# Attention with part of the exponentials on VectorE: batches opened more densely, closed early, and worked in halves

## The chip, the cores and the metric

The kernel runs on one core of a Trainium2 chip. The metric is the device time of one execution in microseconds, the median over several runs. Five engines each work through a list of their own, in order: TensorE (PE, with its weight loads as PEld), VectorE (DVE), ScalarE (ACT), GpSimd (POOL) and SyncE (SP, which issues nearly all DMAs).

## The reference

The input x has 2048 rows of 640 numbers (bf16). Two branches read it and a gate mixes them:

```python
g = sigmoid((x * gate_w).sum(-1, keepdims=True))
# A: attention, 32 heads of 20, scale 20 ** -0.5
q, k, v = heads(x @ wqkv)
p = softmax(einsum("bhqd,bhkd->bhqk", q, k) * scale)
a = merge(einsum("bhqk,bhkd->bhqd", p, v)) @ wo
# B: dense 640 -> 1536 -> 640 with mish
h = x @ w1 + b1
b = (h * tanh(softplus(h))) @ w2
out = g * a + (1 - g) * b
```

The attention has 32 x 2048 x 2048 scores, and each needs an exponential. That is the bulk of the work outside TensorE.

## The kernel before, in words

**How it is tiled.** The queries are cut into four chunks `c` of 512, the heads into eight groups `g` of four. A pair (c, g) is a group of the schedule; there are 33, because the last pair is cut into two of 256 queries. For each group and each of 16 key tiles of 128 keys, the scores of one head fill one PSUM bank: 128 keys x 512 queries in fp32. That is one unit; there are 2048. No maximum is subtracted; a check on the size of q and k, made while the kernel runs, would send it to a second, safe program that is not executed with these inputs.

**Slots.** Three banks make a slot, and 683 slots make the attention. `emit_s` (line 1086) writes a slot's scores (`score_mms`, line 1107, matmuls at line 1117) into one of two sets of three banks, so the scores of slot s + 2 wait until slot s has been read. `emit_e` (line 1128) issues one ScalarE exponential per slot over all its banks (line 1139, PSUM to the ring `ETS` of five slots in bf16). `pv` (line 1349, matmuls at line 1363) multiplies V with the exponentials, four heads at a time, and sums a group's output in one PSUM bank (ACC). When a group's last tile has been multiplied, `group_done` (line 1399) copies ACC to `OUNG` (line 1444), has the row sums inverted (line 1451, with DMAs around it) and scales (line 1412).

**Banks that VectorE takes.** In some slots ScalarE reads only two banks, and VectorE takes the third: `emit_x` (line 1181, instruction at line 1184) turns the scores into 16-bit integers whose bits, read as bf16, are a rough exponential F. Up to four such banks of one group, each of another head, make a batch and lie in a pad, a piece of memory that happens to be free. When the batch is closed (`close`, line 1199), five more VectorE steps follow for the whole batch: two masks (line 1240) split mantissa and exponent E, an affine map of the mantissa (line 1244), its square (line 1249) and the product with F (line 1254), which gives a correction U. TensorE then multiplies V with F, E and U, so one bank taken this way costs three bank passes of a batch in place of one (`emit_off`, line 1319). Pads come from `take_pad`: two of their own (`PADS`), two work areas, and regions lent until their owner needs them: a half of `HB` and the key tiles of the last two head groups (`LENT`, regions k 6 and k 7 of `KT`); later parts of `QT` and `OTN`.

**What sets the order.** Nothing is scheduled on the chip. A planner in the kernel (`attention`) walks through the slots with its own cost for each instruction and writes every engine's list, with semaphore waits between them. Around this change it works as follows.

- `choose(s)` (line 1272) says whether slot s gives a bank to VectorE. Before the change it refuses when the slot before gave one, when VectorE's lag behind ScalarE and its queued work together reach `BEHIND` = 7 us, when too few pads are free, or, for a new batch, when the group's end is nearer than `FILL` + `CHAIN` (5 + 5 us) and the queued work. It takes a unit of the group, of a head that is in neither the slot nor the batch.
- A batch is closed when it has four banks, or when its group has no unit left for it.
- `close` puts the five steps as pieces into one of two lanes; `work(until)` (line 434) picks pieces that fit before the next fixed instruction of VectorE.
- Other work goes between: tasks for the projections (`pack_task`, `pack_end_task`, `v_pair_task`), the dense branch (`h_task` with its eviction at line 901, `mish` with a ScalarE tanh at line 924 and four VectorE steps at line 942, `b_task` evicted at line 957) and the output projection (`p_task`, `part_task`, matmuls at line 974, evictions at line 980). Tasks marked forced are put in at their due slot whatever else waits (line 1666). `fill_up` puts in spare matmuls (line 1642) where TensorE's list would be thin.

Of the kernel before, what the change touches and what calls it, by code (L numbers as in the profile page):

```python
# [9 lines left out]
BF16 = mybir.dt.bfloat16  # L10
I32 = mybir.dt.int32
I16 = mybir.dt.int16
FP16 = mybir.dt.float16
# [24 lines left out]
SLOT = 3  # L38
# [17 lines left out]
WIDE = 0.60  # L56
FAST = 0.335
HALVED = 0.41
LANES = 2
TAKEN = 3.6  # L60
LATE_OFF = 0.8
# [163 lines left out]
def bass_gated_mix__softmax_full_mha__dense_activation_mish__prompt_kernel(  # L225
# [141 lines left out]
    def attention(pl, fast):  # L367
# [831 lines left out]
        def close():  # L1199

            batch = open_batch[0]
            if batch is None or len(batch["evs"]) < len(batch["units"]):
                return
            open_batch[0] = None
            lane = soon[n_batches[0] % LANES]
            n_batches[0] += 1
            y, m = batch["y"], len(batch["units"])
            evs = list(batch["evs"])
            batch["parts"]["F"] = evs[-1]
            got = {}  # L1210
            group = batch["group"]
            ends = max((i for i, v in enumerate(islice(order, 80)) if v[:2] == group), default=0)
            if place[order[0][:2]] < place[group] if order else False:
                ends += NKT * HG
            due = pl.now["act"] + ends / TAKEN * EXP

            def piece(cost, fns, deps, after=None):
                def run():
                    for fn in fns():
                        op = pl.add("dve", fn, deps(), cost=cost * m / BATCH / len(spans(m)) if len(spans(m)) > 1 else cost if m == BATCH else cost * m / BATCH + 0.03)  # L1220
                    after(op)
                lane.append((cost, run, lambda: latest_of(deps()), due))

            def latest_of(ops):
                ops = [op for op in ops if op is not None]
                return max(ops, key=lambda op: op.t1) if ops else None

            def reserve():
                def run():
                    batch["u"], got["u"] = take_pad(batch)  # L1230
                    batch["E"], got["E"] = take_pad(batch)
                lane.append((0.0, run, lambda: None if len(free_pads()) >= 2 else False, due))

            def step(name):
                def after(op):
                    got[name] = op
                return after

            def masked(to, mask):
                return lambda: [lambda e, sp=sp: e.tensor_scalar(  # L1240
                    some_of(batch[to], sp, I16), some_of(y, sp, I16), mask, None, ALU.bitwise_and) for sp in spans(m)]

            def affine():
                return [lambda e, sp=sp: e.tensor_scalar(
                    some_of(batch["u"], sp, FP16), some_of(batch["u"], sp, I16), FIT_AT / 128, FIT_AT + FIT_TO,
                    ALU.mult, ALU.add) for sp in spans(m)]

            def square():
                return [lambda e, sp=sp: e.tensor_tensor(  # L1249
                    some_of(batch["u"], sp, FP16), some_of(batch["u"], sp, FP16), some_of(batch["u"], sp, FP16),  # L1250
                    ALU.mult) for sp in spans(m)]

            def times_f():
                return [lambda e, sp=sp: e.tensor_tensor(
                    some_of(batch["u"], sp, BF16), some_of(batch["u"], sp, FP16), some_of(y, sp, BF16),
                    ALU.mult) for sp in spans(m)]
# [12 lines left out]
            piece(DOUBLE, square, lambda: [got["a"]], step("s"))  # L1269
            piece(DOUBLE, times_f, lambda: [got["s"]], end)  # L1270

        def choose(s):

            late = max(0.0, pl.now["dve"] - pl.now["act"])
            urgent, other = (sum(t[0] for todo in some for t in todo) for some in ((norm, *soon), (blend, bg)))
            if len(order) < SLOT or late + urgent + other >= BEHIND or s - 1 in off:
                return None
            js = [v[3] for v in islice(order, 2)]
            near = list(islice(order, 80))
            batch = open_batch[0]  # L1280
            if batch is None:
                group = near[2][:2]
                ends = max(i for i, v in enumerate(near) if v[:2] == group)
                left = ends / TAKEN * EXP
                before = sum(t[0] for t in blend if t[3] < pl.now["act"] + left)
# [15 lines left out]
            top = NKT  # L1301
# [359 lines left out]
        for step in range(NSLOT + 40):  # L1661
# [227 lines left out]
```

## Time and profile before

| | |
|---|---|
| median of 3 runs | 850.33 us (849.99 to 850.58) |
| the profiled execution | 851.44 us, of which the trace spans 849.6 us |
| granted TensorE clock, mean | 0.991 |
| busy: PE, DVE, ACT | 747.2, 738.8, 825.0 us |
| ScalarE exponentials (line 1139) | 683, of them 403 over three banks and 280 over two |
| banks taken by VectorE (line 1184) | 279 (the last slot has only two banks) |

How to read it: a row of a group view gives line, engine, operation, output <- input, shapes and count, then busy time, the mean length of one instruction, and the idle time of the engine just before, with what ended it. An engine's instructions overlap at their ends, so the busy time of a group is less than count times mean; the distance from start to start is what an instruction costs its engine. The view of windows gives busy time of each engine in a stretch, the granted share of the TensorE clock (PEclk), the busy share of the DMA engines and GB/s. In the timeline a row has start, length, engine, line and what it waited for.

### The profile page before, as it was taken

How to read it: one execution, taken by the hardware profiler on the slowest of the kernel's cores; microseconds unless marked ns; L12 is line 12 of the kernel's file. 1: busy time of each engine (PE TensorE's matmuls, PEld its weight loads, DVE VectorE, ACT ScalarE, POOL GpSimd, SP SyncE). 2: the span in 40 equal slices, each digit the busy share in tenths (PEclk: the TensorE clock that was granted, in tenths of full speed). 3: DMA queues.
4: the chain of work that ended last, by engine and by line, in shares of the span. 5: the costliest groups of instructions: out<-in, count | busy, mean ns of one | idle time of the engine just before them, and what ended most of it. 6: DMA issues, size and time to landing. Idle time of an engine off the chain costs nothing.

```text
span 849.6 us, 16334 instructions
## 1 busy us (share of the span) xinstructions
PE 747.2 (88%) x6813; PEld 265.5 (31%) x6853; DVE 738.8 (87%) x1052; ACT 825.0 (97%) x714; POOL 7.3 (1%) x14
## 2 busy tenths in 40 slices
PE   8889999889888889899888998889998989899884
PEld 3333333233222332233223333333333333233231
DVE  4678788999999998778968899979999999999884
ACT  6999999999999999999999999999999999999983
POOL 3000000000000000000000000000000000000000
PEclk9999999999999999999999999999999999999997
DMA  9721310221223221411111221112212121000001
GB/s 216 96 60 44 105 50 12 73 58 50 67 82 97 79 58 49 125 39 31 33 54 36 65 61 47 30 39 59 76 35 66 44 76 46 10 26 22 18 15 35
DMA packets 78180, 48.47 MB, mean 57 GB/s; under 512 B 23964, under 2 KB 73748, under 8 KB 78052
## 3 DMA queue, kind: packets, MB, share of 16 engines
q1 hardware_dynamic: 75732, 46.87, 20.9%
q8 instruction: 56, 0.92, 0.4%
q10 hardware_dynamic: 2256, 0.47, 0.3%
q0 software_dynamic: 112, 0.01, 0.1%
q14 instruction: 24, 0.20, 0.1%
HBM read 37.64 MB, written 7.52 MB: 53 GB/s over the span
## 4 chain that ended last, share of the span: by engine, by line
ACT 93%; PE 3%; DVE 2%; DMA 1%; issue 0%; SPq 0%; ACTq 0%
ACT ETS L1139 90%; ACT REG L924 2%; PE PS L1117 1%; ACT W2R L924 1%; PE PS L1363 1%; DMA RR<-OUNG 1%; DMA OTN<-in_A_x_dram 1%; PE PS L891 0%; PE PS L974 0%; PE PS L1642 0%; DVE HB L980 0%; PE PS L719 0%; PE PS L772 0%; DVE KT L1249 0%; PE PS L710 0%
## 5 line engine op out<-in xcount | busy, mean ns | idle before, releaser
L1139 ACT ACTIVATE ETS<-PS 128x1536 bf16<-128x1536 f32 (+1 forms) x683 | 807.5, 1507 | 6.2 <-PE PS L1363 3.9
L1117 PE MATMUL PS<-QT,KT 32*128 32x512 bf16 (+1 forms) x2161 | 272.1, 378 | 81.5 <-ACT ETS L1139 65.7
L1363 PE MATMUL PS<-ETS,V_all 128*21 128x512 bf16 (+1 forms) x1818 | 188.1, 379 | 0.3 <-ACT ETS L1139 0.3
L1117 PEld LDWEIGHTS PS<-QT,KT 32*128 32x128 bf16 x2161 | 67.7, 91 | 288.4 <-ACT ETS L1139 251.2
L1363 PEld LDWEIGHTS PS<-ETS,V_all 128*21 128x21 bf16 x1818 | 48.8, 89 | 81.2 <-issue 76.0
L950 PE MATMUL PS<-W2R,HB 128*128 128x320 bf16 x384 | 71.9, 302 | 0.4 <-DVE HB L901 0.2
L1184 DVE TENSOR_SCALAR PADS<-PS 128x512 int16<-128x512 f32 x88 | 60.2, 684 | 12.8 <-PE PS L1117 12.4
L891 PE MATMUL PS<-XB,REG 128*128 128x256 bf16 x360 | 57.6, 279 | 0.9 <-DVE HB L901 0.5
L1184 DVE TENSOR_SCALAR QT<-PS 128x512 int16<-128x512 f32 x56 | 38.4, 685 | 14.0 <-PE PS L1117 13.7
L1184 DVE TENSOR_SCALAR OTN<-PS 128x512 int16<-128x512 f32 x67 | 45.7, 682 | 5.4 <-PE PS L1117 4.8
L901 DVE TENSOR_TENSOR HB<-PS,B1T 128x512 bf16<-128x512 f32 x48 | 32.8, 683 | 10.3 <-PE PS L891 10.0
L950 PEld LDWEIGHTS PS<-W2R,HB 128*128 128x128 bf16 x384 | 29.0, 97 | 36.1 <-issue 25.0
L891 PEld LDWEIGHTS PS<-XB,REG 128*128 128x128 bf16 x360 | 28.3, 98 | 28.6 <-issue 26.3
L1363 PE MATMUL PS<-PADS,V_all 128*21 128x512 bf16 (+1 forms) x278 | 27.6, 372 | 0.6 <-DVE PADS L1240 0.6
L1249 DVE TENSOR_TENSOR PADS<-PADS 128x2048 f16<-128x2048 f16 x23 | 27.9, 1219 | 0.2
L974 PE MATMUL PS<-WOQ,QT 128*128 128x320 bf16 x128 | 25.6, 313 | 0.5 <-issue 0.3
L974 PE MATMUL PS<-WOQ,OTN 128*128 128x320 bf16 x128 | 24.0, 302 | 0.7 <-DVE OUTT L980 0.6
L772 PE MATMUL PS<-REG,XB 128*128 128x160 bf16 (+1 forms) x240 | 24.2, 234 | 0.1
L639 PE MATMUL PS<-XB,REG 128*128 128x512 bf16 x71 | 22.5, 384 | 1.6 <-issue 0.8
L924 ACT ACTIVATE REG<-HB 128x1024 f32<-128x1024 bf16 x18 | 23.8, 1322 | 0.0
L1444 DVE COPY OUNG<-PS 128x512 f32<-128x512 f32 x31 | 21.2, 684 | 2.7 <-PE PS L1363 2.4
L942 DVE SCALAR_TENSOR_TENSOR U<-REG 128x1024 f32<-128x1024 f32 x18 | 21.9, 1218 | 0.8 <-ACT REG L924 0.8
(193 smaller groups left out, 835.5 us busy)
## 6 DMA issues: line engine op xcount, KB each, us to landing
REG<-in_B_w_dram SPq DMA_DIRECT2D x36, 320.0 KB, 3.1
BCT<-SUMS SPq DMA_DIRECT2D x124, 64.0 KB, 2.1
W2R<-in_B_w_dram SPq DMA_DIRECT2D x12, 320.0 KB, 3.3
KT<-KS SPq DMA_DIRECT2D x28, 128.0 KB
QT<-QS SPq DMA_DIRECT2D x112, 20.0 KB
QS<-WOQ SPq DMA_DIRECT2D x16, 128.0 KB, 1.7
KS<-OTN SPq DMA_DIRECT2D x16, 128.0 KB, 1.7
W2R<-in_B_w_dram SPq DMA_DIRECT2D x1, 1920.0 KB, 10.2
```

The lines of the kernel that those rows point to most:

```text
L639: return lambda e, bank: e.matmul(PS[:, bank, :], W[:, f, base:base + P], xt(c)[:, f, :], start=(f == 0), stop=(f == NFT - 1))
L772: return lambda e, bank: e.matmul(PS[:, bank, i * n:(i + 1) * n], xt(t // 4)[:, f, t % 4 * P:(t % 4 + 1) * P], WV[:, f, g * HD:g * HD + n] ...
L891: return lambda e, bank: e.matmul(PS[:, bank, i * HW:(i + 1) * HW], w1b(n1)[:, f, i * P:(i + 1) * P], xt(c)[:, f, cols], start=(f == 0), s ...
L901: ev = dve(lambda e: e.tensor_tensor(hb, PS[:, bank, :].rearrange("p (i t) -> p i t", i=2), bias, ALU.add), [last, b_load, *guarded, *b_re ...
L924: ex = pl.add("act", lambda e: e.activation(U, h, AF.Tanh, scale=0.5, bias=-MISH_AT / 2), [ev, u_free[0]], cost=0.95)
L950: return lambda e, bank: e.matmul(PS[:, bank, 0:HALF], HB[:, hc % 2, f, t * P:(t + 1) * P], W2[:, f, half * HALF:(half + 1) * HALF], start ...
L974: return lambda e, bank: e.matmul(PS[:, bank, 0:HALF], otn(c, g, fast)[:, t * P:(t + 1) * P], WOG[:, g, half * HALF:(half + 1) * HALF], st ...
L1117: op = pl.add("pe", lambda e, i=i, g=real(g), tile=tile, j=j, cols=cols, c=c, of_q=of_q: e.matmul(scores(s)[:, i, cols], KT[32 * j:32 * j ...
L1139: e_op[s] = pl.add("act", lambda e: e.activation(ETS[:, s % NETS, 0:n, :], scores(s)[:, 0:n, :], AF.Exp, scale=SCALE, bias=LIFT if fast el ...
L1184: ev = dve_by(lambda e: e.tensor_scalar(block(batch["y"], n, I16), scores(s)[:, 2, :], SCALE * ULPS, BIAS, ALU.mult, ALU.add), [s_op[s], * ...
L1249: return [lambda e, sp=sp: e.tensor_tensor(some_of(batch["u"], sp, FP16), some_of(batch["u"], sp, FP16), some_of(batch["u"], sp, FP16), AL ...
L1363: lasts[n] = pl.add("pe", lambda e, tile=tile, h=real(g) * HG + j, j=j, src=src[:, cols], of_q=of_q, count=count: e.matmul(PS[32 * j:32 * ...
```

## The change

It touches the planner only; every kind of instruction stays, and the lists come out in another order and number.

1. **Pace.** A slot may give a bank although the slot before did, if few of the last four did (`crowded`); three in a row only where VectorE's queue is under 1.5 us. A new batch is opened as long as 2.5 + 2.5 us, the margin and the queued work fit before the group's end (`FILL` halved, half of `CHAIN`).
2. **Closing.** Where the group's end comes near, an open batch is closed with one, two or three banks.
3. **Halves.** The two products of a batch of four (square and product with F) may run as two instructions of half the size, where the whole would not fit before VectorE's next fixed instruction.
4. **Lent pads.** For forced tasks `ready()` is called from 30 slots before they are due, which withdraws the lent pads k 6 and k 7 from the list of open pads that much earlier.

In the built lists this makes of 279 banks in 71 batches (69 of four, one of two, one of one) 303 banks in 79 batches (68 of four, nine of three, two of two). Of the 68 batches of four, 38 squares and 44 products are issued in halves. ScalarE has 379 exponentials over three banks and 304 over two. VectorE's list grows by 191 instructions. TensorE gets 48 more full-size V matmuls; its spare matmuls of line 1642 go from 67 to 49, and its scores of line 1117 from 2161 to 2154. SP has the same 475 instructions in another order, POOL the same 20 in the same order.

```diff
-FILL = 5.0
+FILL = 2.5
+PACE = 4
+GIVE_BACK = 30
+IDLE = 1.5
+HALF_WORK = 0.60
...
@@ work
+                        halve = len(todo[0]) > 4 and begin + cost > until
+                        if halve:
+                            cost = HALF_WORK
                         if begin + cost <= until and (best is None or begin < best[0] - 0.01):
-                            best = (begin, todo, fn)
+                            best = (begin, todo, fn, halve)
...
+                if best[3]:
+                    todo = best[1]
+                    halves = todo[0][4]
+                    todo.popleft()
+                    todo.extendleft(reversed(halves))
+                    todo.popleft()[1]()
+                    continue
@@ close
-            def piece(cost, fns, deps, after=None):
...
+            def piece(cost, fns, deps, after=None, split=False):
+                def run(some, each, mark):
+                    def go():
+                        for sp in some:
+                            op = pl.add("dve", fns(sp), deps(), cost=each)
+                        if mark:
+                            after(op)
+                    return go
...
+                if split and m == BATCH:
+                    parts = [(0, 1, 0, 2), (1, 2, 0, 2)]
+                    entry += ([(HALF_WORK, run([sp], HALF_WORK, n == 1), after_deps, due) for n, sp in enumerate(parts)],)
+                lane.append(entry)
...
-            piece(DOUBLE, square, lambda: [got["a"]], step("s"))
-            piece(DOUBLE, times_f, lambda: [got["s"]], end)
+            piece(DOUBLE, square, lambda: [got["a"]], step("s"), True)
+            piece(DOUBLE, times_f, lambda: [got["s"]], end, True)
+        def crowded(s, todo):
+            lately = sum(s - i in off for i in range(1, PACE + 1))
+            return s - 1 in off and lately > (1 if todo >= IDLE else 2)
@@ choose
-            if len(order) < SLOT or late + urgent + other >= BEHIND or s - 1 in off:
+            if len(order) < SLOT:
                 return None
...
+            def tight(group, need):
+                ends = max((i for i, v in enumerate(near) if v[:2] == group), default=0)
+                left = ends / TAKEN * EXP
+                before = sum(t[0] for t in blend if t[3] < pl.now["act"] + left)
+                return (late + urgent + before) * CROWD + need + MARGIN >= left
+            batch = open_batch[0]
+            if batch and place[near[2][:2]] >= place[batch["group"]] and tight(
+                    batch["group"], CHAIN * (len(batch["units"]) + 1) / BATCH):
+                close()
+            if late + urgent + other >= BEHIND or crowded(s, late + urgent + other):
+                return None
...
-                if (late + urgent + before) * CROWD + FILL + CHAIN + MARGIN >= left:
+                if tight(group, FILL + CHAIN / 2):
@@ main loop, each step
+            for t in tasks:
+                if t.forced and t.due - GIVE_BACK <= step:
+                    t.ready()
```

More of the change, by code (lines that the diff above doesn't have):

```diff
@@ L1215, in close @@
             due = pl.now["act"] + ends / TAKEN * EXP
-            def piece(cost, fns, deps, after=None):
[L1218 to L1222, printed above, removed]
+            def piece(cost, fns, deps, after=None, split=False):
[6 more added lines that the diff above has]
+                    return go
+                where = spans(m)
+                each = cost * m / BATCH / len(where) + (0.0 if m == BATCH else 0.03)
+                after_deps = lambda: latest_of(deps())
+                entry = (each * len(where), run(where, each, True), after_deps, due)
+                if split and m == BATCH:
+                    parts = [(0, 1, 0, 2), (1, 2, 0, 2)]
+                    entry += ([(HALF_WORK, run([sp], HALF_WORK, n == 1), after_deps, due) for n, sp in enumerate(parts)],)
+                lane.append(entry)
             def latest_of(ops):
@@ L1239, in masked, with affine, square, times_f @@
             def masked(to, mask):
[L1240 to L1244, printed above, removed]
+                return lambda sp: lambda e: e.tensor_scalar(
+                    some_of(batch[to], sp, I16), some_of(y, sp, I16), mask, None, ALU.bitwise_and)
+            def affine(sp):
+                return lambda e: e.tensor_scalar(
                     some_of(batch["u"], sp, FP16), some_of(batch["u"], sp, I16), FIT_AT / 128, FIT_AT + FIT_TO,
[L1246 to L1256, printed above, removed]
+                    ALU.mult, ALU.add)
+            def square(sp):
+                return lambda e: e.tensor_tensor(
+                    some_of(batch["u"], sp, FP16), some_of(batch["u"], sp, FP16), some_of(batch["u"], sp, FP16), ALU.mult)
+            def times_f(sp):
+                return lambda e: e.tensor_tensor(
+                    some_of(batch["u"], sp, BF16), some_of(batch["u"], sp, FP16), some_of(y, sp, BF16), ALU.mult)
             def end(op):
@@ L1282, in choose @@
                 group = near[2][:2]
-                ends = max(i for i, v in enumerate(near) if v[:2] == group)
-                left = ends / TAKEN * EXP
-                before = sum(t[0] for t in blend if t[3] < pl.now["act"] + left)
-                if (late + urgent + before) * CROWD + FILL + CHAIN + MARGIN >= left:
+                if tight(group, FILL + CHAIN / 2):
                     n = place[group] + 1
@@ L1300, in choose @@
             js += [u[3] for u in batch["units"]]
-            top = NKT
             mine = [v for v in near[2:] if v[:2] == group and v[3] not in js and v[2] < tiles(*group) - 1]
```

## The prediction

> **What bounds the kernel now.** I read the page first (shares, chain), then the groups by form, the chain in order of time, the windows of 50 us, the waits, and the timeline where ScalarE stopped. The page:
>
> ```profile
> span 849.6 us, 16334 instructions
> PE 747.2 (88%) x6813; PEld 265.5 (31%) x6853; DVE 738.8 (87%) x1052; ACT 825.0 (97%) x714; POOL 7.3 (1%) x14
> ...
> ACT 93%; PE 3%; DVE 2%; DMA 1%; issue 0%; SPq 0%; ACTq 0%
> ```
>
> ScalarE is busy 97% of the span and holds 93% of the chain. So what a bank costs ScalarE is what moving it is worth, as long as nothing makes ScalarE wait. Two groups by form, and three pieces of the chain in order of time (start, length, what):
>
> ```profile
> L1139 ACT ACTIVATE ETS<-PS 128x1536 bf16<-128x1536 f32 x403 | 637.0, 1680 | 3.4 <-PE PS L1363 1.8 <-PE PS L1117 1.5
> L1139 ACT ACTIVATE ETS<-PS 128x1024 bf16<-128x1024 f32 x280 | 352.2, 1258 | 2.8 <-PE PS L1363 2.1 <-PE PS L1117 0.6
> ...
> 327.48 0.94 ACT W2R L924
> 328.41 77.20 ACT ETS L1139 x67
> 405.61 0.94 ACT REG L924
> ```
>
> The means differ by 1.680 - 1.258 = 0.422 us. In the piece of 67 exponentials 30 are over two banks (counted in the built list), so one over three costs (77.20 + 30 x 0.422) / 67 = 1.341 us and one over two 0.919 us. All of ScalarE's stream is then 403 x 1.341 + 280 x 0.919 + 24 tanh x 0.94 = 820.3 us. The rest of the span is start (the first exponential is at 9.8 us), end, and few waits: 6.2 us before the exponentials, of which 3.9 us behind L1363 lie at the end (below).
>
> VectorE is the next limit, and not evenly:
>
> ```profile
> 300.00:350.00 50.00, 43.38 (x390) 14.12 (x394) 45.56 (x66) 50.00 (x45) 0.00 (x0) 1.00 0.33 94
> 350.00:400.00 50.00, 46.09 (x399) 15.12 (x397) 39.05 (x59) 50.00 (x45) 0.00 (x0) 1.00 0.11 29
> 500.00:550.00 50.00, 44.39 (x383) 16.04 (x379) 48.72 (x65) 50.00 (x45) 0.00 (x0) 1.00 0.16 45
> 600.00:650.00 50.00, 45.31 (x403) 16.88 (x399) 49.25 (x65) 50.00 (x45) 0.00 (x0) 1.00 0.22 60
> 700.00:750.00 50.00, 46.24 (x398) 16.42 (x394) 48.73 (x66) 50.00 (x45) 0.00 (x0) 1.00 0.13 36
> ```
>
> Columns are PE, PEld, DVE, ACT, POOL. VectorE has 39 us of work in one window and 49 in another, and ScalarE is at 50.00 in all: a VectorE that is 98.5% busy (600 to 650) did not stop it.
>
> **The change, part by part.**
>
> *ScalarE.* 24 banks more leave it (303 against 279): 24 x 0.422 = 10.1 us less, 810.2 us of stream. That is the whole gain that the change can bring. Where they come from: before slot 100 seven, slots 100 to 350 ten, 350 to 600 eight, behind it one less.
>
> *VectorE.* What an instruction costs is the distance between starts:
>
> ```profile
> 799.86 0.68 DVE L1184 TENSOR_SCALAR OTN<-PS 128x512 int16<-128x512 f32 x1
> 800.46 0.68 DVE L1412 TENSOR_TENSOR QT<-OUNG,BCT 128x512 bf16<-128x512 f32 x1
> 801.06 1.22 DVE L1249 TENSOR_TENSOR OTN<-OTN 128x2048 f16<-128x2048 f16 x1
> 802.20 0.68 DVE L1184 TENSOR_SCALAR OTN<-PS 128x512 int16<-128x512 f32 x1
> ...
> 836.73 0.62 DVE L1240 TENSOR_SCALAR PADS<-OTN 128x1024 int16<-128x1024 int16 x2
> 837.26 0.62 DVE L1244 TENSOR_SCALAR OTN<-OTN 128x1024 f16<-128x1024 int16 x2
> 837.92 1.03 DVE L1249 TENSOR_TENSOR OTN<-OTN 128x1024 f16<-128x1024 f16 x2
> 838.98 1.03 DVE L1254 TENSOR_TENSOR OTN<-OTN 128x1024 bf16<-128x1024 f16 x2
> ```
> ```profile
> L1249 DVE TENSOR_TENSOR OTN<-OTN 128x1024 f16<-128x1024 f16 x1 | 0.7, 693 | 0.0
> ```
>
> An eviction or a mask over four banks takes 0.60 us, a product 1.14, so about 0.08 less than its length, and a half product 0.693 - 0.083 = 0.61. The tail shows a batch of three: 0.54 per mask or map, 0.95 per product (1.03 - 0.08), and 0.12 more where an instruction follows its own producer (837.26 to 837.92 is 0.66). The sum: 24 evictions 14.4; 82 halved products x (2 x 0.61 - 1.14) = 6.6; nine batches of three x (3 x 0.54 + 2 x 0.95) = 31.7; one batch of four less, -4.1; the small batches about +0.9. Together +49.5 us: 738.8 becomes 788 in a shorter span, 94% busy in place of 87%. Bank for bank that is 2.06 us of VectorE for 0.42 us of ScalarE.
>
> I laid these costs on both built lists between the same evictions. ScalarE against VectorE, us: slots 5 to 100, before 111.8 and 84.0, after 111.5 and 97.2; 100 to 350, before 296.3 and 262.9, after 289.8 and 277.1; 350 to 600, before 310.3 and 283.3, after 306.9 and 303.2. Cut into five, that last stretch has after the change ScalarE 60.6, 60.2, 64.6, 60.1, 61.5 and VectorE 60.1, 57.9, 64.4, 59.1, 61.8. So VectorE's free time goes from 27 to under 4 us there; the cover that hid its work is gone.
>
> *What comes back as waits.* VectorE's list also holds evictions that must wait for TensorE, so it can't be 100% busy. In the three fullest windows above it idles 1.28, 0.75 and 1.27 us of 50, 2.2% on average. If that share stays, each stretch of 50 slots takes 1.022 times its VectorE work or its ScalarE work, whichever is longer: 0.8 + 1.2 + 0.2 + 1.7 = 3.9 us over ScalarE in slots 351 to 601, none elsewhere. With no idle time it is 0.3 us; with 4% it is 10.4 us, of which 2.0 in slots 102 to 300 (at 97% before any idling). I take 3.9, the measured share; halved products make idle gaps smaller, which speaks for less, and the next point for more.
>
> *Two in a row.* 41 times two, 4 times three neighbouring slots give a bank (never before). The scores of slot s + 2 wait for both readers of slot s, and have one exponential of 0.92 in place of 1.34 us to be made in. How tight it is:
>
> ```profile
> 460.40 0.68 DVE L1184 TENSOR_SCALAR PADS<-PS 128x512 int16<-128x512 f32 x1
> ...
> 461.23 0.39 PE L1117 MATMUL PS<-QT,KT 32*128 32x512 bf16 x3 [0.69 <-DVE PADS L1184]
> ```
>
> There the eviction, not ScalarE, released the scores. Before, ScalarE lost 2.1 us to late scores (L1117) in all. Bounds: nothing, to 49 x 0.42 = 20.6 us if every place was just in time. I take it as part of the 3.9 us, since VectorE catches up while ScalarE waits; alone, at 0.06 us a place, it would be 3.
>
> *TensorE.* 24 more passes of a batch at 0.22 to 0.40 us are 5 to 10 us; 18 spare matmuls less give back 5 (L1642: 16.9 us for 57). [...]
>
> ```profile
> 462.00:464.00 2.00, 1.92 (x11) 1.12 (x11) 1.95 (x3) 2.00 (x3) 0.00 (x0) 0.62 0.00 0
> 464.00:466.00 2.00, 2.00 (x14) 0.44 (x12) 1.16 (x2) 1.31 (x2) 0.00 (x0) 0.53 0.00 0
> ...
> 464.84 1.02 ACT L1139 ACTIVATE ETS<-PS 128x1024 bf16<-128x1024 f32 x1 [0.56 <-PE PS L1117]
> 466.27 2.37 ACT L1139 ACTIVATE ETS<-PS 128x1536 bf16<-128x1536 f32 x2 [0.40 <-PE PS L1117]
> ```
>
> The granted clock fell once, to 0.62 and 0.53, and ScalarE waited 0.96 us. [...]
>
> *The end.* ScalarE waits 2.13 and 1.78 us for the last full group:
>
> ```profile
> 824.51 0.40 PE L1363 MATMUL PS<-REG,V_all 128*21 128x256 bf16 x8
> 825.15 2.37 ACT L1139 ACTIVATE ETS<-PS 128x1024 bf16<-128x1024 f32 x2 [2.13 <-PE PS L1363]
> 829.30 7.74 ACT L1139 ACTIVATE ETS<-PS 128x1536 bf16<-128x1536 f32 x6 [1.78 <-PE PS L1363]
> ```
>
> The V matmul at 824.51 waited for that group's last product. In the after list one eviction (slot 675) stands behind this product and no longer before it: 0.6 us earlier. The rest of the end has the same instructions, one of L980 moved across.
>
> *Pads, SP, POOL.* Withdrawing k 6 and k 7 earlier leaves fewer homes; what that costs is already in the count of 303. SP's 475 instructions are the same, reordered with the groups; POOL's list is the same: 0. A group's inversion DMAs could hold a VectorE step; such waits were 3.1 us in all (L1451), the ring of five slots covers them.
>
> **Sum.** -10.1 + 3.9 - 0.6 = -6.8 us. The profiled execution took 851.44 us, 1.1 above the median of 850.33; it would be 844.6, the median 843.5.
>
> **Rivals.**
> (a) The gain stays whole: the halves fill every gap and VectorE idles nowhere. -10.1 + 0.3 - 0.6 gives 839.9. For it: 49.25 of 50 us without a stop. Against: five stretches at 96 to 101%.
> (b) VectorE becomes the bound and takes the gain back: at 4% idle, +10.4 gives 850.0. For it: before, no stretch of 50 slots was over 97%.
> (c) Slower: in the same stretches evictions that wait for TensorE idle VectorE by 5%. Then 1.05 times its work is 15.1 us over ScalarE's, and the time is 854.7. It decides from 4% on. Against it: the fullest windows idle 1.5 to 2.6%.
> (d) The clock falls more often because 18 spare matmuls go: at 0.96 us each it takes seven more drops to eat the gain; three would give 846.4.
>
> [...] (e) By full lengths a halved product costs 2 x 0.693 - 1.217 = 0.17 more and the added work is 62 us and not 49.5; the 12 more, nearly all in full stretches, would give about 853. The rows disagree: starts 0.60 apart at lengths of 0.68.
>
> **How the numbers follow.** Forecast (840.5 to 847) 0.64; (a) 0.12; (b) 0.11, of which a third within 0.2% and a tenth above; (c) 0.09; (d) 0.03, faster; (e) 0.01. A measurement tells 0.2%, 1.7 us, from no change. Faster 0.86, same 0.04, slower 0.10. The range leaves out (c), (e) and the edge below (a): 839.8 to 849.8; the forecast's own is 840.5 to 847.
>
> **What would show it.** Right: 303 rows of L1198 and 304 exponentials over two banks; ScalarE busy some 815 us; VectorE busy near 785; DVE windows from 400 to 700 us at 48.5 and above; ScalarE's waits 3 to 5 us more, spread over the middle. Wrong: windows where ACT falls under 49 with VectorE as releaser, idle time at group ends (L1400 as releaser), or further drops of PEclk.

## The result, and the profile after

The change takes 839.51 us (median; 838.85 to 841.38) against 850.16 for the kernel before, measured beside it: a ratio of the means of 0.9879, interval 0.9862 to 0.9896. The forecast was 843.5 in a range from 839.8 to 849.8, so the gain is 10.7 us by the medians and not 6.8; the median lies 0.3 us under the range's lower end, and its runs reach into the range. The time is that of rival (a), though not for its reasons (see below). The profiled execution took 839.48 us. The head of its page, its chain, and its two groups of exponentials by form:

```profile
span 837.6 us, 16588 instructions
...
PE 748.1 (89%) x6829; PEld 267.2 (32%) x6868; DVE 779.4 (93%) x1243; ACT 815.2 (97%) x714; POOL 7.3 (1%) x14
...
ACT 93%; PE 3%; DVE 2%; DMA 1%; issue 0%; SPq 0%; ACTq 0%
```
```profile
L1153 ACT ACTIVATE ETS<-PS 128x1536 bf16<-128x1536 f32 x379 | 580.4, 1624 | 1.6 <-PE PS L1131 1.4
L1153 ACT ACTIVATE ETS<-PS 128x1024 bf16<-128x1024 f32 x304 | 351.7, 1203 | 0.7 <-PE PS L1131 0.7
```

ScalarE still holds 93% of the chain, with 24 more exponentials over two banks. Their means differ by 0.421 us as before. The idle time in front of the exponentials went from 6.2 us (3.4 + 2.8) to 2.3 (1.6 + 0.7). What fell away is the 3.9 us behind the V matmuls; the 2.1 us behind the scores stayed 2.1. VectorE gained 40.6 us of work. Its windows (PE, PEld, DVE, ACT, POOL, PEclk, DMA):

```profile
20.00:100.00 80.00, 71.85 (x719) 26.46 (x727) 67.97 (x114) 78.56 (x68) 0.00 (x0) 1.00 0.38 73
...
300.00:350.00 50.00, 44.17 (x418) 16.18 (x417) 48.34 (x83) 49.94 (x46) 0.00 (x0) 1.00 0.19 52
350.00:400.00 50.00, 45.87 (x394) 14.16 (x396) 46.15 (x72) 50.00 (x46) 0.00 (x0) 1.00 0.23 69
500.00:550.00 50.00, 47.22 (x414) 17.96 (x411) 48.76 (x77) 50.00 (x45) 0.00 (x0) 1.00 0.23 64
600.00:650.00 50.00, 46.77 (x418) 18.57 (x417) 49.78 (x73) 50.00 (x45) 0.00 (x0) 1.00 0.23 66
700.00:750.00 50.00, 45.19 (x386) 15.61 (x384) 48.46 (x78) 50.00 (x44) 0.00 (x0) 1.00 0.09 25
...
426.60:735.30 308.70, 281.55 (x2472) 103.18 (x2475) 304.58 (x461) 308.68 (x269) 0.00 (x0) 1.00 0.19 52
```

The last row is slots 350 to 600. VectorE works 304.58 of 308.70 us there and ScalarE is busy in all but 0.02. VectorE's lighter windows of before have been filled up.

To see where the 12.0 us between the two spans (849.6 and 837.6) went, I cut each span into four: the start up to the first exponential; ScalarE's stream, with every exponential at its shortest usual distance to the next start (1.330 us over three banks, 0.904 over two, 0.946 for a tanh); the waits, which are what the distances have beyond these; and the tail from the start of the last exponential. All values in us, from the profiled executions. An exponential's record is some 0.3 us longer than its distance to the next (1.624 against 1.330 us), so a start that is a little late is a wait here though ScalarE shows no idle time:

| | banks | start | stream | waits: slots 0-100, 100-350, 350-600, 600-660, behind | tail | span |
|---|---|---|---|---|---|---|
| before | 279 | 9.8 | 811.0 | 2.1, 3.2, 4.3, 1.0, 4.7 | 13.6 | 849.6 |
| after | 303 | 10.2 | 800.8 | 3.3, 3.8, 3.3, 0.9, 0.1 | 15.3 | 837.6 |

The stream gives 10.2 and the end 2.9 (4.6 of waits less, 1.7 of tail more). The middle, from slot 100 to 660, gives 0.5, and the first 100 slots with the start cost 1.6. The spans differ by 12.0 and the medians by 10.7 because the profiled execution of before is 1.1 us slower than its median (851.44 against 850.33): its clock fell once in the middle (0.62 from 462 to 464 us, 0.53 from 464 to 466), and 1.4 us of its waits lie there.

The end after, as the timeline shows it, first VectorE, then ScalarE, then TensorE:

```profile
819.47 0.55 DVE L994 SCALAR_TENSOR_TENSOR HB<-PS,GATE,W2R 128x320 bf16<-128x320 f32 x1 [2.13 <-PE PS L988]
...
823.63 0.55 DVE L994 SCALAR_TENSOR_TENSOR HB<-PS,GATE,W2R 128x320 bf16<-128x320 f32 x1 [0.71 <-PE PS L988]
824.10 0.62 DVE L1265 TENSOR_SCALAR PADS<-OTN 128x1024 int16<-128x1024 int16 x2
...
826.89 1.03 DVE L1278 TENSOR_TENSOR PADS<-PADS,OTN 128x1024 bf16<-128x1024 f16 x2
829.06 0.45 DVE L1468 STREAM_TRANSPOSE BCT<-PS 128x256 f32<-128x256 f32 x1 [1.14 <-PE PS L1400]
...
794.06 29.63 ACT L1153 ACTIVATE ETS<-PS 128x1536 bf16<-128x1536 f32 x25
831.22 0.53 ACT L1794 ACTIVATE PADS<-PS,GATE 128x320 f32<-128x320 f32 x1 [7.54 <-PE PS L988]
...
827.97 0.39 PE L1400 MATMUL PS<-PADS,V_all 128*21 128x256 bf16 x3 [2.05 <-DVE PADS L1278]
829.33 2.50 PE L988 MATMUL PS<-WOQ,QT 128*128 128x320 bf16 x8 [0.33 <-issue]
```

ScalarE runs its last 25 exponentials without the two stops of 2.13 and 1.78 us that it had before, and is done at 823.7. But the last batch's five steps start only at 824.10: they stand in VectorE's list behind output evictions (L994) that wait for TensorE. TensorE waits 2.05 us for the last of them, and what it then multiplies ends the kernel.

### The profile page after: what moved, and what is told of

It is laid out like the page before. It is cut to its first block, busy times and chain, and to the rows that moved or that the text cites. A ratio compares the mean times of both kernels' runs of the same rounds, so it can differ in the third digit from the quotient of the medians.

```text
span 837.6 us, 16588 instructions
## 1 busy us (share of the span) xinstructions
PE 748.1 (89%) x6829; PEld 267.2 (32%) x6868; DVE 779.4 (93%) x1243; ACT 815.2 (97%) x714; POOL 7.3 (1%) x14
## 4 chain that ended last, share of the span: by engine, by line
ACT 93%; PE 3%; DVE 2%; DMA 1%; issue 0%; SPq 0%; ACTq 0%
ACT ETS L1153 90%; ACT REG L938 2%; ACT W2R L938 1%; PE PS L1131 1%; PE PS L1400 1%; DMA RR<-OUNG 1%; DMA OTN<-in_A_x_dram 1%; DVE KT L1198 0%; DVE PADS L1278 0%; DVE PADS L1274 0%; PE PS L584 0%; DVE HB L994 0%; PE PS L733 0%; PE PS L828 0%; DVE OTN L662 0%
## 5 line engine op out<-in xcount | busy, mean ns | idle before, releaser
L1153 ACT ACTIVATE ETS<-PS 128x1536 bf16<-128x1536 f32 (+1 forms) x683 | 796.0, 1437 | 2.3 <-PE PS L1131 2.1
L1400 PE MATMUL PS<-ETS,V_all 128*21 128x512 bf16 (+1 forms) x1798 | 192.2, 378 | 0.3 <-ACT ETS L1153 0.3
L1198 DVE TENSOR_SCALAR PADS<-PS 128x512 int16<-128x512 f32 x101 | 68.7, 682 | 7.3 <-PE PS L1131 7.2
L905 PE MATMUL PS<-XB,REG 128*128 128x256 bf16 x360 | 55.2, 275 | 1.2 <-DVE HB L915 0.6
L1198 DVE TENSOR_SCALAR QT<-PS 128x512 int16<-128x512 f32 x45 | 30.7, 684 | 3.2 <-PE PS L1131 3.1
L1400 PE MATMUL PS<-PADS,V_all 128*21 128x512 bf16 (+1 forms) x294 | 30.9, 379 | 2.1 <-DVE PADS L1278 2.1
L1274 DVE TENSOR_TENSOR PADS<-PADS 128x1024 f16<-128x1024 f16 (+2 forms) x43 | 31.8, 751 | 0.2
L1198 DVE TENSOR_SCALAR OTN<-PS 128x512 int16<-128x512 f32 x45 | 30.8, 685 | 1.2 <-PE PS L1131 1.2
L1198 DVE TENSOR_SCALAR REG<-PS 128x512 int16<-128x512 f32 x43 | 29.3, 683 | 2.2 <-PE PS L1131 2.2
L988 PE MATMUL PS<-WOQ,QT 128*128 128x320 bf16 x128 | 26.7, 312 | 0.8 <-issue 0.3
L988 PE MATMUL PS<-WOQ,OTN 128*128 128x320 bf16 x128 | 23.6, 302 | 0.1
L1274 DVE TENSOR_TENSOR OTN<-OTN 128x1024 f16<-128x1024 f16 (+2 forms) x28 | 23.0, 826 | 0.1
```

The lines of the kernel that those rows point to most:

```text
L905: return lambda e, bank: e.matmul(PS[:, bank, i * HW:(i + 1) * HW], w1b(n1)[:, f, i * P:(i + 1) * P], xt(c)[:, f, cols], start=(f == 0), s ...
L988: return lambda e, bank: e.matmul(PS[:, bank, 0:HALF], otn(c, g, fast)[:, t * P:(t + 1) * P], WOG[:, g, half * HALF:(half + 1) * HALF], st ...
L1153: e_op[s] = pl.add("act", lambda e: e.activation(ETS[:, s % NETS, 0:n, :], scores(s)[:, 0:n, :], AF.Exp, scale=SCALE, bias=LIFT if fast el ...
L1198: ev = dve_by(lambda e: e.tensor_scalar(block(batch["y"], n, I16), scores(s)[:, 2, :], SCALE * ULPS, BIAS, ALU.mult, ALU.add), [s_op[s], * ...
L1274: return lambda e: e.tensor_tensor(some_of(batch["u"], sp, FP16), some_of(batch["u"], sp, FP16), some_of(batch["u"], sp, FP16), ALU.mult)
L1400: lasts[n] = pl.add("pe", lambda e, tile=tile, h=real(g) * HG + j, j=j, src=src[:, cols], of_q=of_q, count=count: e.matmul(PS[32 * j:32 * ...
```

## The experiments

Three theories were set against each other. A: in slots 350 to 600 VectorE is level with ScalarE, its idle time can be used (4.0 us in the expectations; 308.70 less 304.58 is 4.1, or 1.3%), and what goes beyond comes back whole. B, the prediction's own: that idle time is forced, and all added work comes back. C: the waits don't follow VectorE's load. K and V, further down, are on what makes a list with the same work slow.

### How much room VectorE has left

The lists stay those of the changed kernel; one VectorE reduction that nobody reads is put in behind the masks of each batch of four, 23 times in slots 350 to 600 at 512 or at 256 elements, or nine times in slots 5 to 100. Nothing is left out of the computation.

```diff
             def end_e(op):
                 batch["parts"]["E"] = op
+                if m == BATCH and 350 <= now["step"] + 2 < 600:    # dose_early: 5 and 100
+                    keep = pl.now["dve"]
+                    spare[0] = pl.add("dve", lambda e: e.tensor_reduce(
+                        JUNK[:, 0:1], block(y, 0)[:, 0:512], AX.X, ALU.max), [*evs, spare[0]], cost=0.0)
+                    pl.now["dve"] = keep                          # dose_half: 0:256
```

The full dose, 23 x 0.60 = 13.8 us (each is 0.68 us long in the trace; 0.08 less is an estimate from the evictions, which have that length and start 0.60 apart):

> The changed kernel with 23 VectorE instructions of 0.60 us that nobody reads (a maximum over 512 numbers), each behind the second mask of a batch of four in slots 350 to 600; the planner does not know of them, so every list stays as it is. 13.8 us of work in a stretch where the changed kernel leaves VectorE 4.0 us idle of 307.1. Theory A (VectorE and ScalarE are level there, and idle time of VectorE is nearly all free): 13.8 - 4.0 = about 10 us slower than the changed kernel, near 849. Theory B (part of the idle time is forced by evictions that wait for TensorE, as the prediction's 2.2% had it): all 13.8 us, near 853. Theory C (ScalarE alone bounds, VectorE's lag is taken up by the ring and by slots without a bank): under 4 us, below 844.

Measured: 850.31 us, ratio 0.9996 (0.9986 to 1.0006). The gain of the whole change is gone.

The half dose, 23 x 0.33 = 7.7 us (0.41 us long in the trace, less the same 0.08):

> The same with half the size: 23 instructions of 0.33 us, 7.7 us in slots 350 to 600. Theory A: 7.7 - 4.0 = 3.7 us slower than the changed kernel, near 843.2. Theory B: 7.7, near 847. Theory C: under 1.5 us.

Measured: 843.98 us, ratio 0.9927 (0.9911 to 0.9944).

The early dose, 9 x 0.60 = 5.4 us:

> The same instructions of 0.60 us behind 9 batches in slots 5 to 100, where VectorE is idle 16.7 of 110.9 us: 5.4 us of work. Theories A and C: the free time takes it up, within 1 us of the changed kernel. Theory B, in the form that each unplanned instruction delays the next eviction and so ScalarE at once: 3 to 5 us slower.

Measured: 840.82 us, ratio 0.9880 (0.9864 to 0.9897).

Windows of the full dose, and a place in its timeline (VectorE, TensorE, ScalarE; lines are up to seven further down than after):

```profile
450.00:500.00 50.00, 43.02 (x387) 14.46 (x385) 49.00 (x75) 48.07 (x43) 0.00 (x0) 1.00 0.14 36
600.00:650.00 50.00, 45.02 (x400) 17.93 (x398) 49.88 (x74) 48.70 (x43) 0.00 (x0) 1.00 0.22 62
```
```profile
483.25 0.69 DVE L1280 TENSOR_TENSOR PADS<-PADS 128x1024 bf16<-128x1024 f16 x1
483.86 0.55 DVE L995 SCALAR_TENSOR_TENSOR OUTT<-PS,GATE,XB 128x320 bf16<-128x320 f32 x1
484.32 0.68 DVE L1456 TENSOR_TENSOR QT<-OUNG,BCT 128x512 bf16<-128x512 f32 x1
484.92 0.68 DVE L1200 TENSOR_SCALAR QT<-PS 128x512 int16<-128x512 f32 x1
...
485.75 0.61 PE L1133 MATMUL PS<-QT,KT 32*128 32x512 bf16 x6 [0.70 <-DVE QT L1200]
...
482.67 2.36 ACT L1155 ACTIVATE ETS<-PS 128x1024 bf16<-128x1024 f32 x2 [0.38 <-PE PS L1133]
486.19 4.20 ACT L1155 ACTIVATE ETS<-PS 128x1024 bf16<-128x1024 f32 x4 [1.15 <-PE PS L1133]
```

ScalarE falls under 49 in windows where VectorE is no busier than in the changed kernel (49.00 and 49.88 here, 48.99 and 49.78 there, with ScalarE at 50.00 in both). The place shows the path: the eviction of a bank (L1200 at 484.92) comes late behind three other steps, the scores that need the bank wait, and ScalarE waits 1.15 us for them. The waits in slots 350 to 600 rise from 3.3 to 8.3 and 15.6 us, the times by 4.5 and 10.8. From the half dose to the full one 6.1 us more of work cost 6.3 us more of time, 1.03 each; drawn back to no cost, that line begins at 7.7 - 4.5 / 1.03 = 3.3 us. So some 3.3 of VectorE's 4.1 idle us were free, and the next us comes back whole. Part of it comes through the clock: it fell to half for 3.4 us once in the middle of the half dose and three times in that of the full one (a window of 50 us at 0.97 in the one, three in the other), and 0.7 and 2.1 us of the waits lie in these falls; without them the waits still grow by 5.9 us for 6.1. The line goes through two points whose ratios have intervals of some 1.4 and 0.9 us to either side, so 3.3 is a rough figure. The measured times lie between A (849 and 843.2) and B (853 and 847), nearer to A; C (below 844, and under 1.5 us for the half dose) falls. The early dose goes into a stretch (24 to 123 us) where VectorE has time to spare: 12.0 us from 20 to 100 us alone (80 less 67.97, after the change). By the medians it costs 1.3 us for 5.4, by the ratios (0.9880 against 0.9879) nothing: it is absorbed, and B, which had 3 to 5 us there, doesn't hold.

### The end

The changed kernel, with the open batch closed at slot 677; its banks stay 303:

```diff
+CLOSE_AT = 677
...
+            if fast and step + 2 == CLOSE_AT:
+                close()
```

> The changed kernel, with one more call of close at slot 677: the last batch of three, taken in slots 670, 672 and 675, is closed there and not when its group has ended. Its chain (3.9 us, 824.10 to 827.97 in the changed kernel's trace, behind the end of ScalarE's stream at 823.7) then lies beside ScalarE's last exponentials, where VectorE waits 2.13, 1.26, 0.54 and 0.71 us for TensorE. Theory: the chain is on the path that sets the end, so 2.5 to 3.5 us faster than the changed kernel, near 836.5. Rival: V matmuls and the last output tiles take its place, under 1 us.

Measured: 834.35 us, ratio 0.9809 (0.9793 to 0.9825), the fastest of all runs: 5.2 us under the changed kernel, more than was expected. Its VectorE, ScalarE and TensorE at the end:

```profile
816.83 0.62 DVE L1266 TENSOR_SCALAR PADS<-OTN 128x1024 int16<-128x1024 int16 x2
...
819.98 1.02 DVE L1279 TENSOR_TENSOR PADS<-PADS,OTN 128x1024 bf16<-128x1024 f16 x2
...
823.75 0.45 DVE L1469 STREAM_TRANSPOSE BCT<-PS 128x256 f32<-128x256 f32 x1
...
825.78 0.53 ACT L1797 ACTIVATE PADS<-PS,GATE 128x320 f32<-128x320 f32 x1 [2.52 <-PE PS L989]
...
825.43 0.72 PE L989 MATMUL PS<-WOQ,QT 128*128 128x320 bf16 x4 [0.42 <-DVE QT L1475]
```

The five steps now lie beside the last exponentials (ScalarE ends at 823.3), and the wait behind them is 2.52 in place of 7.54 us; the tail is 10.4 in place of 15.3. The windows show what can make it more than the moved steps. First the changed kernel, then this one:

```profile
824.00:826.00 2.00, 0.60 (x6) 0.12 (x6) 1.97 (x8) 0.00 (x0) 0.00 (x0) 0.68 0.20 58
826.00:828.00 2.00, 0.03 (x4) 0.04 (x7) 1.88 (x4) 0.00 (x0) 0.00 (x0) 0.50 0.00 0
828.00:830.00 2.00, 1.67 (x17) 0.96 (x19) 0.88 (x3) 0.00 (x0) 0.00 (x0) 0.50 0.00 0
```
```profile
820.00:825.00 5.00, 4.35 (x54) 1.76 (x51) 3.24 (x9) 3.26 (x3) 0.00 (x0) 1.00 0.18 52
825.00:830.00 5.00, 0.74 (x5) 0.31 (x4) 2.30 (x5) 0.53 (x1) 0.86 (x1) 1.00 0.31 92
```

While TensorE waited for the late batch, its clock fell to half, and the closing matmuls ran slowly (eight of L988 in 2.50 us, where this run has four in 0.72). With the batch early there is no such wait and no fall before the last matmul.

The same line put into the kernel before (279 banks):

> The kernel before, with the open batch closed at slot 677 and nothing else (279 banks). Theory (the last batch's late closing costs the same in both kernels, since its five steps stand behind the last evictions): the waits of 4.7 us behind slot 660 and the tail of 13.6 us shrink together by 3 to 5 us, 846 to 848. Rival (in before the end is set by the wait for the last full group's product, which the closing at 677 does not move): less than 1 us, 849.5 or more.

Measured: 847.08 us, ratio 0.9964 (0.9951 to 0.9977), 3.6 us less than before. The tail shrinks from 13.6 to 10.3, but the waits behind slot 660 stay (4.9): those two stops belong to the last full group's product, and the changed kernel's list is what removed them. The theory is right on the time and the tail and wrong on the waits; the rival is right on the waits and wrong on the time. With the closing at 677 in both kernels the change is worth 12.7 us (847.08 less 834.35).

### One part undone at a time

The changed kernel with one part as it was before. For the pace, no two neighbouring slots give a bank:

```diff
-            return s - 1 in off and lately > (1 if todo >= IDLE else 2)
+            return s - 1 in off
```

> The changed kernel with the old pace: never two neighbouring slots. 290 banks. By the stream: 11 x 0.422 = 4.6 us faster than before, near 845.5 (845 if the end gains as in the changed kernel, 2.9 us, then near 843). If two in a row cost ScalarE waits, this kernel has fewer waits in the middle than the changed one.

Measured: 841.02 us, ratio 0.9888 (0.9872 to 0.9905), faster than both forecasts. Its waits are 2.1 us fewer than the changed kernel's, but in the first 100 slots (1.2 against 3.3), not in the middle. For the closing and opening near a group's end:

```diff
-FILL = 2.5
+FILL = 5.0
...
-            if batch and place[near[2][:2]] >= place[batch["group"]] and tight(
+            if False and batch and place[near[2][:2]] >= place[batch["group"]] and tight(
...
-                if tight(group, FILL + CHAIN / 2):
+                if tight(group, FILL + CHAIN):
```

> The changed kernel with the old opening (5 + 5 us before the group's end) and no early closing; dense pace, halves and pads as changed. 284 banks. By the stream: 5 x 0.422 = 2.1 us faster than before, near 848. Rival: opening and closing only move batches about, and the time stays within 3 us of the changed kernel.

Measured: 846.75 us, ratio 0.9951 (0.9934 to 0.9968): about what the stream gives, and not the rival's. For the halves:

```diff
-                if split and m == BATCH:
+                if False and split and m == BATCH:
```

> The changed kernel without halved products. The planner then gives 297 banks (303 with halves). By ScalarE's stream alone: 18 banks more than before x 0.422 = 7.6 us faster than before, 2.5 us slower than the changed kernel, near 842. If halves are what keeps VectorE's gaps small, ScalarE's waits grow too: 844 or more.

Measured: 848.58 us, ratio 0.9977 (0.9957 to 0.9997), with runs from 843.98 to 851.68: the second case, more waits. For the pads, returned when they were before:

```diff
-GIVE_BACK = 30
+GIVE_BACK = -1
```

> The change without its fourth part (lent pads are returned when they were before; 297 banks in place of 303). By ScalarE's stream alone, 6 banks at 0.427 us are +2.6 us: 842. If the earlier return is also what keeps forced work from coming late, the waits grow beyond 11.3 us and the time is over 844. If it only shifts banks between stretches and VectorE was the limit there: no more than 840.5.

Measured: 850.65 us, ratio 1.0001 (0.9989 to 1.0014): over 844, as the second case has it, but whether forced work came late these runs don't show. And the edits of the closing and of the halves together, which leaves the dense pace and the returned pads:

> As the one with the old opening and closing, and without halves: the dense pace with pads given back earlier, alone. 287 banks: 8 x 0.422 = 3.4 us faster than before by the stream, near 846.8. If the dense pace without halves makes evictions late, ScalarE's waits eat this: 849 or more.

Measured: 845.62 us, ratio 0.9938 (0.9920 to 0.9957), 1.2 under what the stream gives. All of them in the same four pieces (start and tail as one; us). Pieces and span are those of the profiled execution, which for the old closing and for pace and pads alone was the slowest of four (849.41 and 846.93):

| | banks | stream | waits | start + tail | span | median |
|---|---|---|---|---|---|---|
| after | 303 | 800.8 | 11.3 | 25.5 | 837.6 | 839.5 |
| old pace | 290 | 806.3 | 9.1 | 23.6 | 839.0 | 841.0 |
| pace and pads alone | 287 | 807.6 | 12.4 | 25.0 | 845.1 | 845.6 |
| old closing | 284 | 808.9 | 14.8 | 23.9 | 847.5 | 846.8 |
| no halves | 297 | 803.3 | 18.1 | 24.1 | 845.6 | 848.6 |
| pads as before | 297 | 803.3 | 14.1 | 29.1 | 846.6 | 850.7 |
| after, closed at 677 | 303 | 800.8 | 11.0 | 20.5 | 832.3 | 834.4 |

The stream follows the banks each time; the time doesn't. Undoing the pace gives up 5.5 us of stream and loses 1.5; undoing the pads or the halves gives up 2.5 and loses 11.1 or 9.1. What undoing costs, summed over the four parts, is some 29 us, against a gain of 10.7: a single edit makes a new list, with its own waits and its own end. So these runs don't share the gain out among the parts. They show how far two lists can differ by what is not work: median less stream is 34.7 us with the old pace, 38.7 after and 47.4 with the old pads (before: 39.7, from the 850.73 measured beside the last runs; 33.6 with the closing at 677).

With the old pads the excess is at the end and in the waits. VectorE there, and the window behind its last exponential, which ends at 829.0:

```profile
828.95 0.55 DVE L994 SCALAR_TENSOR_TENSOR HB<-PS,GATE,W2R 128x320 bf16<-128x320 f32 x1 [0.79 <-PE PS L988]
829.41 0.62 DVE L1265 TENSOR_SCALAR REG<-OTN 128x1024 int16<-128x1024 int16 x2
```
```profile
830.00:840.00 10.00, 5.26 (x32) 2.14 (x33) 6.40 (x17) 0.53 (x1) 0.36 (x1) 0.54 0.09 27
```

It is the end of the changed kernel over again, with the clock at 0.54 for 10 us: 3.7 us more of tail, 2.8 more of waits, 2.5 of stream. These 9.0 us hold for the profiled execution of 848.53 us, the fastest of ten; the others, up to 852.71, had granted clocks down to 0.982 in place of its 0.991.

Without the halves the excess is in the middle. TensorE and VectorE of that run, and windows of 2 us:

```profile
588.20 0.39 PE L1131 MATMUL PS<-QT,KT 32*128 32x512 bf16 x3 [0.61 <-DVE OTN L1198]
...
587.38 0.68 DVE L1198 TENSOR_SCALAR OTN<-PS 128x512 int16<-128x512 f32 x1
```
```profile
586.00:588.00 2.00, 1.19 (x14) 0.41 (x10) 2.00 (x5) 2.00 (x3) 0.00 (x0) 1.00 0.11 32
588.00:590.00 2.00, 1.11 (x8) 0.36 (x8) 2.00 (x4) 1.58 (x3) 0.00 (x0) 1.00 0.03 9
590.00:592.00 2.00, 1.85 (x12) 0.78 (x12) 1.62 (x4) 2.00 (x3) 0.00 (x0) 0.51 0.00 0
592.00:594.00 2.00, 2.00 (x15) 0.25 (x11) 1.18 (x2) 0.87 (x2) 0.00 (x0) 0.50 0.33 91
```

VectorE is full, its evictions come late, the scores wait for them, TensorE is busy 1.19 and 1.11 of 2 us; then the clock is at half, and now TensorE is full and ScalarE starves (0.87 of 2). There is lateness at a whole clock too: waits of 1.6 and 1.7 us at 316 and 319 us. Whether the clock or the lateness makes most of the loss, the next run was to tell.

### Clock or lateness

Without the halves, and with more spare matmuls in thin stretches:

```diff
-STREAM = 0.48
-SPUN = 0.6
+STREAM = 0.56
+SPUN = 0.68
```

> The change without the halves (297 banks), and with the planner's two bounds for spare matmuls raised (0.48 to 0.56 and 0.60 to 0.68), so that thin stretches of TensorE's list are filled; nothing else differs from the run without halves, which took 848.6 us with runs scattered from 844.0 to 851.7. Theory K (the scatter and most of the loss of that run are half-clock windows that follow thin stretches of TensorE): granted clock at 0.995 or above, waits before exponentials near 11 us in place of 18.1, and 842 to 844 us with little scatter. Theory V (whole products leave VectorE too coarse, so its evictions come late whatever TensorE has to do): 847 to 850 again, waits near 18 us, most of them between slots 100 and 600. If the spare matmuls themselves get in the way of scores: above 850.

Measured: 846.95 us, ratio 0.9960 (0.9947 to 0.9973), runs from 846.74 to 848.27. The scatter of 7.7 us is down to 1.5 and the clock up to between 0.992 and 0.996, about as theory K has it (0.995 or above); but the time falls by 1.6 us only, and the waits are 22.9 us. It is also more of another list than was expected: 298 banks, and in the trace 110 more matmuls of scores, which the planner repeats to fill, besides 8 more spare ones. Its longest wait behind a late step, VectorE, TensorE and ScalarE in the timeline:

```profile
493.50 1.21 DVE L1278 TENSOR_TENSOR REG<-REG,QT 128x2048 bf16<-128x2048 f16 x1
...
494.77 0.40 PE L1400 MATMUL PS<-REG,V_all 128*21 128x512 bf16 x4 [2.04 <-DVE REG L1278]
...
495.61 2.37 ACT L1153 ACTIVATE ETS<-PS 128x1024 bf16<-128x1024 f32 x2 [3.47 <-PE PS L1400]
```

A whole product ends late, and the V matmuls that need it stand in TensorE's list ahead of those that read the oldest of the five places in the ring of exponentials. The next exponential must write that place, and ScalarE waits 3.47 us; its scores were there (the last scores before it start at 491.25). That is lateness by a whole product, near theory V, though by the ring and not by an eviction. For this list lateness is the larger part: the waits that begin in its two falls of the clock are 5.0 of 22.9 us.

For the list without the halves the question stays open. Its times go with its mean clock, from 843.98 us at 0.992 to 851.68 at 0.977, so 4.6 of the 9.1 us between its median and the changed kernel are there only in runs with a lower clock, and 2.5 are stream. But what thins TensorE's work before a fall is, in the windows above, VectorE's lateness. No run here parts the two.

Last, the version closed at 677 with VectorE's queue bound at 8 in place of 7 us (305 banks):

> The changed kernel with the closing at slot 677 (834.35 us) and the bound on VectorE's queue raised from 7 to 8 us: 305 banks in place of 303, by the stream -0.85 us. Theory A (VectorE is level with ScalarE in slots 350 to 600, so what is added there comes back whole): no gain, 834 to 836. Theory C (the waits don't follow VectorE's load): 833.5.

Measured: 844.10 us, ratio 0.9940 (0.9918 to 0.9961): 9.8 us slower than with 7, for two banks more. Both theories missed. The closing at 677 does not bring the last batch forward as it did there: its square starts only at 826.70, behind an output eviction that waits 1.47 us for TensorE. It has 6.5 us more of waits, 4.0 more of tail and the clock near half in the middle (0.66 from 457 to 462 us, 0.68 from 742 to 747), once so (windows of its trace):

```profile
452.00:454.00 2.00, 0.84 (x10) 0.20 (x7) 1.97 (x3) 2.00 (x3) 0.00 (x0) 1.00 0.00 0
454.00:456.00 2.00, 1.13 (x14) 0.42 (x14) 2.00 (x5) 1.38 (x2) 0.00 (x0) 1.00 0.15 41
456.00:458.00 2.00, 1.57 (x13) 0.36 (x9) 2.00 (x4) 2.00 (x3) 0.00 (x0) 0.76 0.00 0
458.00:460.00 2.00, 2.00 (x9) 0.84 (x9) 1.46 (x2) 1.75 (x2) 0.00 (x0) 0.50 0.02 4
```

## Why the prediction was right in its direction and off in its size

*ScalarE*: right. 10.1 us forecast, 10.2 measured.

*VectorE*: right. Its work in slots 350 to 600 was forecast at 303.2 us and ScalarE's at 306.9; the trace has 304.6 and 308.7. Five of the six windows from 400 to 700 us are above 48.5 (the first has 48.18). Over the whole kernel 785 to 788 us were forecast and 779.4 came, so it was priced some 6 to 9 us too high outside this stretch; which steps these are stays open. The half products cost the 0.61 us that were taken. By the full lengths of rival (e) the stretch would have held some 12 us more; (e) is out: in the full dose the half product at 483.25 is 0.69 us long and the next instruction starts 0.61 us later.

*What comes back as waits*: this step failed. It took the 2.2% that VectorE idled in its fullest windows of before as a share that it must idle, and put 3.9 us on slots 351 to 601. VectorE idled 1.3%, and the waits there fell by 1.0 us; 1.4 us of the waits before, by the same measure, were the clock's fall near 462 us, which the changed kernel's profile doesn't have; so some 0.4 came back. The idle share of an engine that nobody waits for was no lower bound here. The doses put the bound at some 0.8 us in 309 (4.1 less 3.3). Rivals (b) and (c) named the right mechanism and the wrong place of its edge: it took 13.8 us of added work, the full dose, to reach the 850 that (b) gave.

*Two in a row*: the first 100 slots wait 1.2 us more, with three waits of 0.4 to 0.8 us between 29 and 44 us. Two of them follow slots 14 to 16, which all give; the third is at no such place, and the other three places where three slots in a row give have none over 0.3 us. So whether neighbouring slots cause them is not shown. The kernel with the old pace waits 2.1 us less there, under the 3 us named for this effect alone.

*The end*: the second step that was off. One eviction behind the last product was to give 0.6 us. Both stops (3.9 us by the rows) went and the tail grew by 1.7; net 2.9. The forecast followed one product and not the list behind it; that the last batch's steps stood behind waiting output evictions was in the built list, and the closing at 677 shows what it cost: 5.2 us here. It cost 3.6 in the kernel before too, so most of this loss is not the change's.

*Rival (d)*: its price holds (0.62 and 0.53 over 2 us each are 3.4 us at half rate; in the run without halves the time moves by (851.68 - 843.98) / 15 = 0.5 us for each 0.001 of mean clock, so 1.0 us for such a fall, which takes 0.002). Its cause doesn't: with 18 spare matmuls fewer the profiled execution has no fall in the middle.

*Rival (a)*: its 839.9 is close to the 839.5 measured, but by luck. VectorE did not work without idling; the end gave 2.3 us more than (a) has, and the start and the first 100 slots took 1.6.

So the forecast missed by 5.2 us of span: -4.9 in the waits of slots 350 to 600, -2.3 at the end, -0.1 in the stream, +2.1 elsewhere, of which 1.6 at the start. Why this list waits 11.3 us where three lists with fewer banks wait 14 to 18 is explained only place by place; no rule for it was found, and the runs leave that open.

## What to carry to other kernels

The idle time of an engine that isn't the bound need not be a tax (some 3.3 of VectorE's 4.1 us were free here): to learn how much of it can be used, add unread work to that engine with the order unchanged, at two sizes, and read off where the time begins to rise. When a planner writes the order, price the work that an edit moves, but give the rest (waits, the tail) a spread from lists that differ by little; here it was 12.7 us wide (34.7 to 47.4) between lists whose work on the bounding engine differs by 8. And read the last 20 us by themselves: what stands behind a waiting instruction there can be cheap to move, as the one line that closed the last batch was in both kernels that were run with and without it.

## What the runs showed of the hardware

The clock fell to half behind stretches in which TensorE still worked about half of the time and more. It was busy 58% of 4 us (1.19 + 1.11, run without the halves) in one place and 49% (0.84 + 1.13, run with the bound at 8) in another before the clock was at half (0.51 and 0.50 from 590 to 594 us in the one, 0.50 from 458 to 460 us in the other); its gaps were 0.4 to 0.6 us in the first. In the kernel before, TensorE was busy 1.56 and 1.25 of 2 us ahead of the fall that the prediction shows (70%), and its longest gap was 0.69 us:

```profile
458.00:460.00 2.00, 1.56 (x15) 0.58 (x13) 1.82 (x4) 2.00 (x3) 0.00 (x0) 1.00 0.02 3
460.00:462.00 2.00, 1.25 (x14) 0.32 (x11) 2.00 (x3) 2.00 (x3) 0.00 (x0) 1.00 0.16 45
```

The busy share alone doesn't decide it: in the changed kernel TensorE was busy 2.64 of 4 us from 236 to 240 us (66%), less than the 70% before that fall, and the clock stayed whole (1.00 there and up to 248 us). The list without the halves had mean clocks from 0.977 to 0.992 from run to run, and its time went with them over 7.7 us.
